# The 32-partition loads of v issued from ScalarE's queue

## The chip, the core and the metric

The kernel runs on one core of a Trainium2 chip. The core has a matrix engine (TensorE, PE in the rows; its weight loads are PEld), three engines for elementwise work (VectorE = DVE, ScalarE = ACT, GpSimd = POOL) and SyncE (SP), which here does nothing but issue transfers. Each engine takes its own instructions strictly in order and waits on semaphores for the others. Transfers between DRAM and the on-chip memory run on 16 DMA engines; an engine that issues a transfer only starts it. The metric is the device time of one execution, in microseconds.

## The reference, cut to what matters

```python
def _attn_ref(q, k, v):                 # 4 batches, 8 heads, 768 positions, 64 per head
    k_sum = k.reshape(B, H, nb, block, D).max(axis=3)      # 24 blocks of 32 positions
    v_sum = v.reshape(B, H, nb, block, D).mean(axis=3)
    scores_l = scale * np.matmul(q, k.transpose(0, 1, 3, 2))
    mask_l = np.abs(pos[:, None] - pos[None, :]) < 16
    scores_s = scale * np.einsum('bhsd,bhnd->bhsn', q, k_sum) + np.log(block)
    scores_all = np.concatenate([np.where(mask_l, scores_l, -1e9), scores_s], axis=-1)
    a = softmax(scores_all)
    return np.matmul(a, np.concatenate([v, v_sum], axis=2))

def _moe_ref(x, w_in, w_spatial, b_spatial, w_out):        # x: 4 x 768 x 512
    h = np.maximum(x @ w_in, 0.0)
    u, v = h[..., :512], h[..., 512:]
    v_n = (v - mean(v)) / np.sqrt(var(v) + 1e-06)
    v_s = np.einsum('ts,bsd->btd', w_spatial, v_n) + b_spatial[None, :, None]
    return (u * v_s) @ w_out
```

Each query sees the 15 positions on either side of it and all 24 block summaries; the result goes through a gated layer that also mixes positions.

## The kernel before

The attention is cut into 24 groups: 4 batches, 3 chunks of 256 query positions, 2 groups of four heads. A chunk is four blocks of 64 queries. For such a block the keys and values stand as 120 rows: 64 positions, 24 block summaries, and 32 further positions (the window reaches 16 past the block on either side). The value tile `ve` of a group therefore has 120 partitions: 0 to 63 are loaded from DRAM (256 KB), 64 to 87 hold the block means, which ACT writes, and 88 to 119 are loaded from DRAM (128 KB). Two such tiles, `ve0` and `ve1`, are used in turn, one for each group of heads, so a load into one has to wait until the product that reads it (the matmuls at L501, tile `x`) is done for the group before.

For each group PE makes the scores (`s`, L441), DVE and ACT the softmax (`p`: DVE L457, ACT's exponentials L461, DVE or POOL the division L471), PE transposes (`t`, L482), ACT or DVE copies (`pt`), and PE forms `x` from `pt` and `ve`. The dense work stands between: `pv` and `pu` are the two halves of the first layer, `sp` and `q` the mixing of positions, `po` the last layer; all are L543 in the rows. `arena` holds the mixing weights, which in the later batches come back from a DRAM scratch (`scr`) piece by piece; `vt` is v transposed, from which DVE forms block sums (`vs_in`, L407) that PE transposes (`vmp`, L411).

All instructions are collected with a cost and a priority in a `Plan`, whose `order()` lays them out on the engines by the costs; they are then issued in the order of the planned starts, and each engine keeps that order. A transfer is entered by `dma(...)`, booked on SP. Its semaphore is one of eight lanes (DMAHW0 to DMAHW7 in the order's rows), handed out in turn; a transfer also waits until the transfer that had its lane before has landed. In the rows of the order, `[waits ...]` names the semaphores that an instruction waits for, without their values. Where a transfer waits for a lane on which the transfer eight places earlier ran, that lane is the one it takes over.

Of the kernel before, what the change touches and what calls it, by code (L numbers as in the profile page):

```python
# [25 lines left out]
QB = 64  # L26
BPU = 4
CH = QB * BPU
NCH = S // CH
WIN = 16  # L30
# [41 lines left out]
class Plan:  # L72
# [11 lines left out]
    def add(self, engs, fn, pri, w=(), r=(), port=False, xfer=0):  # L84


        op = Op()
        op.engs = engs if isinstance(engs, dict) else dict([engs])
        op.fn, op.pri, op.users, op.n = fn, pri + SHIFT.get(self.label, 0), [], len(self.ops)
        op.label = self.label  # L90
        op.port, op.xfer = port, xfer
        op.ready = op.start = op.end = 0
        after = set()
        for x in r:
            after.update(self.wrote.get(x, ()))
        for x in w:
            after.update(self.wrote.get(x, ()))
            after.update(self.read.get(x, ()))
        for x in w:
            self.wrote[x], self.read[x] = [op], []  # L100
        for x in r:
            self.read.setdefault(x, []).append(op)
        op.after = after
        op.bufs = list(dict.fromkeys(x for x in (*w, *r) if isinstance(x, Buf)))
        for x in (*w, *r):
            if isinstance(x, Buf) and not x.ops and x.tag in self.TURNS and x.args[4][:2] not in self.OUT_OF_TURN :
                self.turn.setdefault(x.tag, []).append(x)
                self.late.add(x)
            if isinstance(x, Buf) and op not in x.ops[-1:]:
                x.ops.append(op)  # L110
        self.ops.append(op)
        return op
# [77 lines left out]
def tile_local_summary_attention_gmlp(ctx: ExitStack, tc: tile.TileContext, qT, kext, vpad, vnat, vT, w_in, w_sp, b_rep, w_out, out):  # L190
    nc = tc.nc
    plan = Plan()
    add = plan.add
# [57 lines left out]
    qd = [const.tile([P, 2, BPU, QB], F32, name=f"qd{i}") for i in range(2)]  # L251
    ve = [const.tile([KW, BPU, 2 * P], F32, name=f"ve{g}") for g in range(2)]

    def dma(out_, in_, kb, pri, w=(), r=(), issue=420, rate=RATE):
        add(("SP", issue), lambda e: nc.sync.dma_start(out=out_() if callable(out_) else out_, in_=in_() if callable(in_) else in_), pri, w, r, xfer=kb * 1024 / rate)  # L255

    def eng(e):
        return dict(DVE=nc.vector, POOL=nc.gpsimd)[e]
# [9 lines left out]
    def split32(src, hi, lo, name, pri, key):  # L268

        n = src.shape[-1]  # L270
        st = Buf(moe, [P, GW], F32, "g", name)
        dma(lambda: st.t[:, :n], src, n * 0.5, pri, w=[st])
        add(("ACT", act_ns(n)), lambda e: nc.scalar.copy(out=hi, in_=st.t[:, :n]), pri, w=[key + "h"], r=[st])
        add(two_ns(n), lambda e: eng(e).tensor_sub(out=lo, in0=st.t[:, :n], in1=hi), pri, w=[key + "l"], r=[st, key + "h"], port=True)

    def split64(st, so, f, fo, src, hi, lo, pri, key, on_pe=False, at=0):

        if src.dtype != I64:
            n = src.shape[-1]
            dma(lambda: st.t[:, so:so + n], src, n * 0.5, pri, w=[(st, so), st])  # L280
            add(("ACT", act_ns(n)), lambda e: nc.scalar.copy(out=hi, in_=st.t[:, so:so + n]), pri, w=[key + "h"], r=[(st, so), st])
            add(two_ns(n), lambda e: eng(e).tensor_sub(out=lo, in0=st.t[:, so:so + n], in1=hi), pri, w=[key + "l"], r=[(st, so), st, key + "h"], port=True)
            return
# [6 lines left out]
        here = plan.label  # L290
        mark("l", key)
        dma(raw, src.bitcast(I32), n, pri + at, w=[kr], r=[st])
        plan.label = here

# [125 lines left out]
    def v_load(b, c, g, buf, pri):  # L420
        s0 = c * CH
        fs = slice(2 * g * P, 2 * (g + 1) * P)
        dma(ve[buf][:QB], vpad[b, s0:s0 + CH, fs].rearrange("(i p) f -> p i f", p=QB), 256, pri, w=[f"vea{buf}"], issue=620, rate=RATE_64)
        dma(ve[buf][SEG:],
            vpad[b, s0 + QB:s0 + QB + CH, fs].rearrange("(i p) f -> p i f", p=QB)[:2 * WIN], 128, pri, w=[f"veb{buf}"], issue=620, rate=RATE_32)

    p_sb, pt_sb = {}, {}

# [444 lines left out]
    def attention(*pair):  # L873
# [4 lines left out]
        def values(i, pri):  # L878
            mark("v", i)
            v_load(*group(i), pri - 4 + off("v", i))  # L880
# [120 lines left out]
WIRE, RATE, RATE_64, RATE_32 = 1900, 355.0, 215.0, 195.0  # L1001
# [58 lines left out]
```

## Time and profile before

| | us |
|---|---|
| median of 3 runs (398.48 to 401.46) | 398.81 |
| the profiled execution | 398.37 |
| span of its instructions | 396.6 |
| PE busy | 385.3 (97%) |
| DVE busy | 277.7 (70%) |
| ACT busy | 227.8 (57%) |
| POOL busy | 76.2 (19%) |
| all transfers, 90 MB on one data queue | 68.5% of 16 engines |

The profiled execution is 1.8 us longer than its span and 0.44 us below the median. The span begins with the first instruction; times of the rows are counted from there. PE begins with the scores of the first groups while the weights are still arriving, works in pieces until about 64 us, and from then on hardly pauses. Busy shares of PE include matmuls that keep its clock up (`warm`, up to 30 us).

### The profile page before, as it was taken

What the parts mean: (1) busy time and instruction counts of PE and PEld (TensorE: products, weight loads), DVE (VectorE), ACT (ScalarE), POOL (GpSimd) and SP (SyncE); (2) the same over time, 40 slices, a digit from 0 to 9 for tenths busy, and PEclk for the clock granted to TensorE, in tenths of its full rate; (3) what the DMA queues carried; (4) which work ended last, traced back from release to release, by engine and by line L of the source; (5) the groups of instructions that cost most, each with busy time, mean ns of one, the idle gap of its engine ahead of it and who ended that gap; (6) DMA issues with size and microseconds to landing.
All of it is one profiled execution on the core that took longest, in us unless ns stands there. A gap on an engine that the chain in (4) does not pass through costs nothing.

```text
span 396.6 us, 9130 instructions
## 1 busy us (share of the span) xinstructions
PE 385.3 (97%) x3372; PEld 335.6 (85%) x3372; DVE 277.7 (70%) x871; ACT 227.8 (57%) x672; POOL 76.2 (19%) x115
## 2 busy tenths in 40 slices
PE   8889998999999999999999999999999999999996
PEld 8657776888899888888998888889998888889985
DVE  3878998989899517999989553577797710687720
ACT  2789998679475625777473743543564821452221
POOL 4244686310001004334012000031000000510000
PEclk9989999999999999999999999999999999999999
DMA  8999999957596846699999910318897110089712
GB/s 284 296 400 335 327 249 266 362 190 206 182 354 237 224 161 232 204 298 328 339 328 361 260 43 0 135 62 323 301 355 245 56 57 0 28 305 364 284 62 99
DMA packets 34284, 90.64 MB, mean 229 GB/s; under 512 B 3264, under 2 KB 15040, under 8 KB 30912
## 3 DMA queue, kind: packets, MB, share of 16 engines
q1 hardware_dynamic: 34240, 90.06, 68.5%
q8 instruction: 27, 0.44, 0.5%
q14 instruction: 17, 0.14, 0.1%
HBM read 73.40 MB, written 16.65 MB: 227 GB/s over the span
## 4 chain that ended last, share of the span: by engine, by line
PE 74%; DMA 13%; DVE 7%; ACT 2%; SPq 1%; issue 1%; POOL 0%; DVEq 0%; ACTq 0%
PE po L543 17%; PE q L543 13%; PE pu L543 13%; PE pv L543 12%; PE sp L543 6%; DMA arena<-scr 4%; PE x L501 4%; PE t L482 4%; PE s L441 4%; DMA vt<-in_vT_dram 3%; DMA qd<-in_qT_dram 2%; DMA k<-in_kext_dram 2%; SPq L255 1%; DMA scr<-ct 1%; ACT p L461 1%
## 5 line engine op out<-in xcount | busy, mean ns | idle before, releaser
L461 ACT ACTIVATE p<-p,sums 128x120 f32<-128x120 f32 x192 | 73.5, 386 | 11.0 <-DVE sums L457 10.9
L457 DVE CUSTOM_DVE_ANT_0 p<-s,mask 128x120 f32<-128x120 f32 x192 | 41.9, 276 | 9.5 <-PE s L441 9.4
L543 PE MATMUL pu<-xh,win_h 128*128 128x256 f32 (+1 forms) x128 | 44.0, 344 | 0.0
L543 PE MATMUL pu<-xh,win_l 128*128 128x256 f32 (+1 forms) x128 | 43.1, 337 | 0.0
L543 PE MATMUL pu<-xl,win_h 128*128 128x256 f32 (+1 forms) x128 | 43.0, 336 | 0.0
L543 PE MATMUL po<-arena,gt 128*128 128x512 f32 (+1 forms) x168 | 40.6, 385 | 0.0
L543 PE MATMUL pv<-win_h,xh 128*128 128x512 f32 x96 | 39.2, 408 | 0.0
L543 PE MATMUL pv<-win_h,xl 128*128 128x512 f32 x96 | 37.6, 391 | 0.0
L543 PE MATMUL pv<-win_l,xh 128*128 128x512 f32 x96 | 37.5, 391 | 0.0
L543 PE MATMUL q<-arena,vnh 128*128 128x384 f32 x144 | 37.4, 340 | 0.1
L461 ACT ACTIVATION_READ_ACCUMULATOR p<-p,sums 128x1 f32 x192 | 36.3, 189 | 0.0
L543 PEld LDWEIGHTS po<-arena,gt 128*128 128x128 f32 x168 | 30.4, 188 | 6.0 <-issue 0.2
L582 POOL TENSOR_SCALAR mv<-mv 128x1 f32<-128x1 f32 x24 | 9.3, 386 | 135.2 <-DVE mv L578 134.5
L577 DVE BATCH_NORM_STATS2 mv<-vf 128x6 f32<-128x512 f32 x24 | 16.4, 683 | 23.1 <-ACT vf L574 23.0
L638 ACT ACTIVATE u<-pu 128x512 f32<-128x512 f32 (+1 forms) x32 | 15.6, 491 | 28.3 <-PE pu L543 28.2
L543 PE MATMUL q<-arena,wo_hl 128*128 128x384 f32 x144 | 29.2, 336 | 0.4 <-DMA arena<-scr 0.4
L261 ACT COPY pt<-t 120x512 f32<-120x512 f32 x38 | 21.8, 584 | 13.0 <-PE t L482 12.8
L482 PE MATMUL t<-ident,p 128*120 128x128 f32 x192 | 28.1, 278 | 1.1 <-POOL p L471 0.9
L482 PEld LDWEIGHTS t<-ident,p 128*120 128x120 f32 x192 | 22.5, 138 | 6.8 <-POOL p L471 2.2
L501 PEld LDWEIGHTS x<-pt,ve 120*64 120x64 f32 x768 | 23.6, 138 | 4.6 <-issue 3.1
L543 PEld LDWEIGHTS pu<-xh,win_h 128*128 128x128 f32 x128 | 24.3, 189 | 3.0 <-issue 0.2
L441 PE MATMUL s<-k,qd 64*64 64x120 f32 x768 | 23.9, 267 | 2.7 <-DMA qd<-in_qT_dram 2.0
(152 smaller groups left out, 872.2 us busy)
## 6 DMA issues: line engine op xcount, KB each, us to landing
arena<-scr SPq DMA_DIRECT2D x21, 1152.0 KB, 6.3
k<-in_kext_dram SPq DMA_DIRECT2D x16, 544.0 KB, 7.8
qd<-in_qT_dram SPq DMA_DIRECT2D x24, 256.0 KB, 7.9
ve<-in_vpad_dram SPq DMA_DIRECT2D x24, 256.0 KB, 8.2
out_dram<-ob SPq DMA_DIRECT2D x23, 256.0 KB, 2.0
arena<-scr SPq DMA_DIRECT2D x5, 1024.0 KB, 7.7
vt<-in_vT_dram SPq DMA_DIRECT2D x12, 384.0 KB, 4.1
scr<-ct SPq DMA_DIRECT2D x12, 384.0 KB, 4.3
```

The lines of the kernel that those rows point to most:

```text
L255: add(("SP", issue), lambda e: nc.sync.dma_start(out=out_() if callable(out_) else out_, in_=in_() if callable(in_) else in_), pri, w, r, ...
L261: (nc.scalar.copy if e == "ACT" else nc.vector.tensor_copy)(out=out_, in_=in_)
L441: nc.tensor.matmul(out=ps[a].t[r * QB:(r + 1) * QB, i * KW:(i + 1) * KW], lhsT=qt[hs, r, i], rhs=kts[r].t[hs, g * SEG:g * SEG + KW], start ...
L457: add(("DVE", 205), lambda e, i=i, mi=mi, a=a, pt=pt, k=k: nc.vector.tensor_tensor_reduce(out=at(pt, i), in0=ps[a].t[:, i * KW:(i + 1) * K ...
L461: add(("ACT", 380), lambda e, i=i, pt=pt, k=k: nc.scalar.activation(out=at(pt, i), in_=at(pt, i), func=AF.Exp, scale=-1.0, bias=st.t[:, 0, ...
L482: nc.tensor.transpose(out=ps.t[:KW, i * P:(i + 1) * P], in_=pt.t[:, i * KW:(i + 1) * KW], identity=ident)
L501: nc.tensor.matmul(out=x.t[a * D:(a + 1) * D, r * CH + n * QB:r * CH + (n + 1) * QB], lhsT=ve[buf][:, n, o:o + D], rhs=tt[a].t[:KW, n * P ...
L543: nc.tensor.matmul(out=ps.t[:, :n], lhsT=x, rhs=y, start=(first and j == i == 0), stop=(j == last and i == 2), skip_group_check=skip)
L577: nc.vector.bn_stats(out=mv.t[:, 2:], in_=vf.t)
L582: nc.gpsimd.tensor_scalar_add(out=mv.t[:, 1:2], in0=mv.t[:, 1:2], scalar1=EPS_LN)
L638: add(("ACT", act_ns(n)), lambda e: nc.scalar.activation(out=u.t[:, f, ts], in_=ps.t[:, :n], func=AF.Relu), pri, w=[(u, f, c)], r=[ps, u])
```

## The change

The function `dma` gets a parameter `queue`, and the second of the two loads in `v_load`, the one of 32 partitions and 128 KB, is issued by ACT (`nc.scalar`) and no longer by SP. The plan still books it on SP with the same costs, so the planned starts are what they were, and the instruction is put into ACT's order at its planned start.

```diff
-    def dma(out_, in_, kb, pri, w=(), r=(), issue=420, rate=RATE):
-        add(("SP", issue), lambda e: nc.sync.dma_start(out=out_() if callable(out_) else out_, in_=in_() if callable(in_) else in_), pri, w, r, xfer=kb * 1024 / rate)
+    def dma(out_, in_, kb, pri, w=(), r=(), issue=420, rate=RATE, queue=nc.sync):
+        add(("SP", issue), lambda e: queue.dma_start(out=out_() if callable(out_) else out_, in_=in_() if callable(in_) else in_), pri, w, r, xfer=kb * 1024 / rate)
@@ v_load
         dma(ve[buf][SEG:],
-            vpad[b, s0 + QB:s0 + QB + CH, fs].rearrange("(i p) f -> p i f", p=QB)[:2 * WIN], 128, pri, w=[f"veb{buf}"], issue=620, rate=RATE_32)
+            vpad[b, s0 + QB:s0 + QB + CH, fs].rearrange("(i p) f -> p i f", p=QB)[:2 * WIN], 128, pri, w=[f"veb{buf}"], issue=620, rate=RATE_32, queue=nc.scalar)
```

24 transfers leave SP's order and stand in ACT's; on PE, DVE and POOL nothing moves. Since the lanes are handed out in the order of issue over both queues, which lane a transfer takes, and which earlier one it so waits for, changes for most transfers behind the first few.

The first place is ACT's order in batch 1, chunk 2, in the softmax of the second group of heads (`p1_2_1_0` and `p1_2_1_1` are its two score tiles, `xh1_01_1` takes the result of the chunk before; rows with + are of after, with - of before).

```order
 L461 ACTIVATE p1_2_1_0_1570,sums_115<-p1_2_1_0_1570,sums_115 128x120 [waits DVE_49,Activation_49]
+L255 DMA ve0_140<-in_vpad_dram 32x4x256 [waits DMAHW7_49,DMAHW5_49]
 L461 ACTIVATE p1_2_1_0_1570,sums_115<-p1_2_1_0_1570,sums_115 128x120 [waits DVE_49] x3
+L255 DMA ve1_141<-in_vpad_dram 32x4x256 [waits DMAHW7_49,DMAHW1_49,PE_49]
 L461 ACTIVATE p1_2_1_1_1583,sums_115<-p1_2_1_1_1583,sums_115 128x120 [waits DVE_49,Activation_49]
 L461 ACTIVATE p1_2_1_1_1583,sums_115<-p1_2_1_1_1583,sums_115 128x120 [waits DVE_49] x3
-L523 CAST xh1_01_1_1339<-x1_1_1_1502 128x2x256 [waits PE_49]
+L523 CAST xh1_01_1_1339<-x1_1_1_1502 128x2x256
```

Two loads now stand among the exponentials. The load of `ve1` takes over lane 7, for which it has to wait.

The second place is SP's order at the same time; `scr8` is a store of weights to the scratch, `qd0` a load of queries, `k2_0` and `k2_1` keys of the next batch.

```order
 L255 DMA scr8_137<-wo_hl_128 128x2x512 [waits DMAHW6_49,DVE_49]
 L255 DMA ve0_140<-in_vpad_dram 64x4x256 [waits DMAHW7_49,PE_49]
-L255 DMA ve0_140<-in_vpad_dram 32x4x256 [waits DMAHW0_49]
-L255 DMA ve1_141<-in_vpad_dram 64x4x256 [waits DMAHW1_49,PE_49]
-L255 DMA ve1_141<-in_vpad_dram 32x4x256 [waits DMAHW2_49]
-L255 DMA qd0_138<-in_qT_dram 128x512 [waits DMAHW3_49,PE_49]
-L255 DMA k2_0_1622<-in_kext_dram 128x1088 [waits DMAHW4_49]
-L255 DMA k2_1_1631<-in_kext_dram 128x1088 [waits DMAHW5_49]
-L255 DMA k2_2_1639<-in_kext_dram 128x1088 [waits DMAHW6_49,PE_49]
-L255 DMA k2_3_1651<-in_kext_dram 128x1088 [waits DMAHW7_49]
+L255 DMA ve1_141<-in_vpad_dram 64x4x256 [waits DMAHW0_49,PE_49]
+L255 DMA qd0_138<-in_qT_dram 128x512 [waits DMAHW2_49,DMAHW1_49,PE_49]
```

The two small loads are gone from SP's order. The transfer that holds lane 7 until it has landed is SP's load of `ve0` with 64 partitions, in the second row, in both kernels; before, `k2_3` took the lane over from it, eight transfers later.

The third place is ACT's order in batch 1, chunk 0, near the end of the stage in which the weights arrive (`xh0_2_0` takes the last result of batch 0, `vmp1_0` block means of batch 1).

```order
 L574 ACTIVATE vf0_2_911<-pv0_2_768 128x512
 L273 CAST arena_125<-ws3_700 128x768 [waits DMAHW0_49]
-L523 CAST xh0_2_0_943<-x0_2_0_886 128x512 [waits PE_49]
+L255 DMA ve0_140<-in_vpad_dram 32x4x256 [waits DMAHW3_49,DMAHW1_49,PE_49]
+L523 CAST xh0_2_0_943<-x0_2_0_886 128x512
 L413 ACTIVATE ve0_140<-vmp1_0_913 24x4x128 [waits PE_49]
 L461 ACTIVATE p1_0_1_0_966,sums_115<-p1_0_1_0_966,sums_115 128x120 [waits DVE_49] x3
+L255 DMA ve1_141<-in_vpad_dram 32x4x256 [waits DMAHW5_49,PE_49]
 L261 COPY pt1_0_0_0_992<-t1_0_0_0_976 120x512 [waits PE_49,Activation_49]
```

On SP the load of `ve0` with 32 partitions stood four transfers behind that of `vt1_2`; now it is on the other queue.

## Rows read from the trace of the kernel before

**Rows 1.** The page: engines with busy time, share of the span and instructions; then the DMA queues with packets, MB and the time of their packets as a share of 16 engines.

```profile
PE 385.3 (97%) x3372; PEld 335.6 (85%) x3372; DVE 277.7 (70%) x871; ACT 227.8 (57%) x672; POOL 76.2 (19%) x115
...
q1 hardware_dynamic: 34240, 90.06, 68.5%
```

**Rows 2.** Who waited for whom, PE alone: total us, times, longest.

```profile
PE s L441 <- DMA qd<-in_qT_dram: 2.0, 1, 2.0
...
PE vmp L411 <- DVE vs_in L407: 1.4, 1, 1.4
...
PE x L501 <- DMA ve<-in_vpad_dram: 0.5, 1, 0.5
...
PE q L543 <- DMA arena<-scr: 0.4, 1, 0.4
PE t L482 <- DVE p L471: 0.2, 1, 0.2
```

**Rows 3.** Stretches: from and to, length, busy time and instructions of PE, PEld, DVE, ACT, POOL, then the granted clock, the share of the DMA engines and GB/s.

```profile
30.00:40.00 10.00, 9.12 (x154) 7.24 (x147) 8.55 (x43) 9.95 (x36) 4.32 (x5) 1.00 1.07 330
40.00:50.00 10.00, 9.89 (x128) 7.54 (x127) 9.49 (x33) 9.92 (x35) 6.15 (x5) 1.00 1.03 333
50.00:60.00 10.00, 9.49 (x130) 7.38 (x131) 9.83 (x34) 9.31 (x29) 8.71 (x7) 1.00 1.07 245
60.00:70.00 10.00, 8.56 (x67) 6.92 (x66) 8.78 (x30) 8.89 (x28) 5.92 (x7) 1.00 1.04 271
...
167.00:175.00 8.00, 8.00 (x141) 7.44 (x138) 7.16 (x29) 4.64 (x17) 1.51 (x3) 1.00 0.96 309
202.00:213.00 11.00, 10.57 (x65) 9.72 (x64) 10.10 (x39) 7.34 (x27) 3.03 (x3) 1.00 1.02 357
278.00:288.00 10.00, 10.00 (x165) 9.51 (x164) 7.27 (x38) 5.62 (x23) 0.00 (x0) 1.00 0.93 308
```

**Rows 4.** The chain that ended last, in order of time, at the end of the stage in which the weights arrive: start, length, what.

```profile
51.80 11.51 DMA vt<-in_vT_dram
...
63.33 0.96 DVE vs_in L407
...
64.43 0.28 PE vmp L411
```

**Rows 5.** DMA issues of the stretch 58.5 to 60: line, size, median us from issue to landing; and SP's timeline there (start, length, what).

```profile
ve<-in_vpad_dram SPq DMA_DIRECT2D x1, 256.0 KB, 8.1
ve<-in_vpad_dram SPq DMA_DIRECT2D x1, 128.0 KB, 8.2
...
58.60 1.25 SPq L255 DMA_DIRECT2D ve<-in_vpad_dram  x2
```

**Rows 6.** All instructions on the tile `ve`: the issues on SP, with ns of one, shortest, median and longest; and SP's timeline at one issue of 128 KB that had waited for its lane.

```profile
L255 SPq DMA_DIRECT2D ve<-in_vpad_dram x48: 327/601/1927, 4.5 to 304.2; - x48
...
46.95 0.33 SPq L255 DMA_DIRECT2D ve<-in_vpad_dram  x1
```

**Rows 7.** SP's timeline around 104, and the issue of the first of these four loads with its time to landing.

```profile
104.40 3.40 SPq L255 DMA_DIRECT2D ve<-in_vpad_dram  x4
...
ve<-in_vpad_dram SPq DMA_DIRECT2D x1, 256.0 KB, 6.7
```

**Rows 8.** ACT's timeline at the place of the first piece of order: the first exponential of `p1_2_1_1`, the end of the fourth, and the cast behind it.

```profile
108.99 0.38 ACT L461 ACTIVATE p<-p,sums 128x120 f32<-128x120 f32 x1
...
110.41 0.19 ACT L461 ACTIVATION_READ_ACCUMULATOR p<-p,sums 128x1 f32 x1
110.51 0.57 ACT L523 CAST xh<-x 128x512 fp32r<-128x512 f32 x1
```

**Rows 9.** DVE's timeline right behind, and PE's transposes of the same tiles.

```profile
110.92 0.17 DVE L466 TENSOR_SCALAR sums<-sums 128x9 f32<-128x9 f32 x1
111.12 0.20 DVE L467 RECIPROCAL sums<-sums 128x8 f32<-128x8 f32 x1
111.25 0.64 DVE L524 TENSOR_TENSOR xl<-x,xh 128x512 fp32r<-128x512 f32 x1
111.80 1.22 DVE L471 TENSOR_TENSOR p<-p,sums 128x480 f32<-128x480 f32 x2
...
113.41 1.04 PE L482 MATMUL t<-ident,p 128*120 128x128 f32 x8
```

**Rows 10.** The stretch from 167: ACT's timeline at the place of a small load, the chain that ended last, and DVE's timeline with its idle time in brackets.

```profile
167.09 0.51 ACT L703 CAST ct<-ct 128x384 fp32r<-128x384 f32 x1
...
167.67 5.87 DMA scr<-ct
...
173.66 0.56 DVE L700 TENSOR_TENSOR ct<-w,w 128x384 f32<-128x384 f32 x1 [0.77 <-DMA scr<-ct]
...
180.89 1.19 PE t L482 x8
```

**Rows 11.** The chain that ended last around 202 to 213.

```profile
199.12 0.60 SPq L255
...
202.01 10.77 DMA arena<-scr
...
212.92 1.11 PE q L543 x5
```

**Rows 12.** The issue of a piece of `arena` at 278.28 with its time to landing, and PE's first matmul that reads it.

```profile
arena<-scr SPq DMA_DIRECT2D x1, 1152.0 KB, 9.1
...
287.69 0.51 PE L543 MATMUL q<-arena,vnh 128*128 128x384 f32 x2
```

## The prediction

> **What bounds the kernel now.** I read the page's engine lines first, then PE's own waits, then the stretches, then the chain that ended last wherever PE had waited. PE is busy for 385.3 of 396.6 us [rows 1], and the list of its waits is short: the waits on transfers and on DVE that it names add to about 4.5 us in the whole execution [rows 2]. From about 64 us on PE runs without a pause in almost every stretch. The time is therefore PE's work plus the pauses put into it: whatever delays PE by a microsecond after 64 us is paid in full, and a faster queue can win back only pauses that exist. Up to 70 us the second limit is the transfers: the DMA engines are at a share of 1.03 to 1.07 for 40 us, while ACT is at 9.95 and 9.92 of 10 between 30 and 50 [rows 3]. That stage ends on a transfer: `vt` is issued at 51.80, lands 11.51 later, DVE reduces it in 0.96, and PE, which had paused 1.4 for it, goes on at 64.43 [rows 2, 4].
>
> **What the change removes.** SP loses 24 issues. At the median of 601 ns that is 14.4 us of SP's time [rows 6], but SP is not what lasts: its transfers wait for lanes, for buffers that PE still reads, or for the backlog. At 51.80 the backlog is 11.5 us [rows 4]; a transfer that is issued half a microsecond earlier lands where the bytes ahead of it let it land. One wait of PE is on `ve` itself, 0.5 us in the first stage [rows 2]; the small load may now land earlier there, but PE then only waits longer for `vt` at 64.43. Removed: 0 us, and with the issue that stands on the chain at 199.12 (0.60) up to 0.35 at one place, counted below.
>
> **What it adds to ACT: the issue.** No row shows an issue on ACT. The nearest are the same loads on SP: 0.33 us where SP had just waited and nothing stood before it, 0.60 as the median, 1.93 at worst [rows 6]. Below nothing is excluded, since ACT's sequencer has one more thing to do. I take 0.33, because on ACT the loads stand alone between computations. In the first stage four of them fall where ACT is full, two near 34 to 37 us and two near 48 to 50: 4 x 0.33 = 1.3 us later. The cover is PE's pause of 1.4 before 64.43 [rows 2]: the delayed work of ACT, DVE and PE has to be done before `vt` lands, and just fits. So 0 at 0.33; above 0.36 each further 0.1 costs 0.4. Elsewhere ACT has 43% idle time, and an issue costs nothing unless the exponentials behind it are awaited.
>
> **What it adds to ACT: the waits.** Each load waits on ACT for its buffer, for its lane's last transfer, and for the earlier load of the same tile; everything behind it on ACT waits too. I went through the 24 places and compared, in the trace, when ACT reaches the place with when the awaited things had come. At 23 of them they had come, or come within some 0.7 us where nobody waits for ACT. The other is the first piece of order, among the exponentials of batch 1, chunk 2. The load of `ve1` takes over lane 7 from SP's 64-partition load of `ve0`. That was issued at 104.40 and took 6.7 us, so it landed at 111.1 [rows 7]. ACT reaches the place at 108.99 [rows 8]. With the issue of 0.33 behind it ACT goes on at 111.4: 2.4 us late. Behind it are four exponentials, whose sums are ready at 110.6 now and 113.0 then. DVE's L466 began at 110.92 [rows 8, 9], so 0.3 is free there, and 2.1 remains; but DVE's `xl` at 111.25 needs ACT's cast at 110.51, which will end at about 113.5, so L471 begins near 114.1 instead of 111.80 and its two halves end near 114.7 and 115.3. PE begins the transposes at 113.41, 1.04 us for the eight, four for each half [rows 9]: it will begin at 114.8 and reach the second four at 115.4 instead of 113.9. That is 1.5 to 1.6 us of pause, and 0.1 more at the next pair of tiles, whose exponentials are late by the same amount: **1.7**. Bounds: 1.0 if the landing comes 0.6 earlier, 2.6 if it comes later because the other queue now takes a share, and the issue costs 0.60.
>
> **What it adds to the transfers.** In the rows all data stand on one queue, q1 [rows 1], and they land in order of issue. A second queue lets the small load run beside what is waiting on the first, so 128 KB are moved ahead of a backlog that they used to close. The small load itself is then early, which nobody needs; what was ahead of it is late. The price is 128 KB at the rate of the stretch, or the distance between two landings. At 58.60 the pair landed at 58.60 + 8.1 and 59.25 + 8.2, 0.7 apart (59.25 is the second issue of the two in 1.25 us) [rows 5]; 128 KB at 271 GB/s are 0.48 [rows 3].
> - At 64.43: the load that is issued at 59.25 now will be issued by ACT near 60, while `vt` is still under way until 63.3. **0.6** (0 to 0.7).
> - At 173.5: DVE waits 0.77 for a landing, issued at 167.67 [rows 10]. ACT is free from 167.6 to 170.4 and will issue its load of `ve0` there, ahead of it. 128 KB at 309 GB/s are 0.42 [rows 3]. The chain runs from that landing over DVE to PE's transposes at 180.89, for which PE waited 0.2 already [rows 2, 10]. **0.5** (0 to 0.8).
> - At 212.9: the piece of `arena` issued at 202.01 lands 10.77 later and PE waited 0.4 for it [rows 2, 11]. The load of `ve0` used to stand behind it and will be issued by ACT near 203.8: 128 KB at 357 GB/s are 0.37 [rows 3]. The issue taken from SP at 199.12 can give 0.35 back. **0.3** (-0.35 to 0.65).
> - At 287.7: the piece issued at 278.28 lands at 287.4 and is read at 287.69 [rows 12], 0.3 to spare; the small load comes near 284.3 and needs 0.43 at 308 GB/s [rows 3]. **0.2** (0 to 0.5).
>
> What a page says of this: the Trainium skill, "DMA: Bandwidth & Descriptors", section "Queues, rings and completion order", has each DMA engine take turns between the queues that have work, a packet at a time. With one data queue before, no row shows it. By that rule the four terms hold at their full price; if the engines served the queues strictly by time of issue, all four would be 0.
>
> **The sum.** 0.6 + 1.7 + 0.5 + 0.3 + 0.2 = 3.3 us of new pauses on PE, 0 for the issues. From the profiled execution of 398.37 that gives 401.7. Against the median of 398.81, which is 0.44 above that execution, it is 0.7% more. Less than 1%, about 4 us, is hardly told from no change by runs of this kernel, whose three runs lie between 398.48 and 401.46.
>
> **The rivals.**
> - *The second queue carries its loads for nothing.* The share of the DMA engines is 1.07 both at 330 and at 245 GB/s [rows 3], so a full share is not a full rate, and two queues could overlap better. Then the two small loads near 47 to 49 no longer stand ahead of `vt`, which could land up to 1.4 earlier (2 x 0.7), as much as PE's pause there; the four terms are 0, and the wait of ACT keeps its 1.7: 398.4 - 1.4 + 1.7 = **398.7**. Without the wait of ACT it is 397.0. A gain of over 1% would need more than 3.6 us, nearly all of PE's waits in rows 2, in one go. For it: the uneven rates. Against it: the uneven rates also follow the kinds of transfers. The same page of the Trainium skill, section "Issuing engines are not separate DMA queues", says that transfers of all issuing engines run on the same 16 DMA engines and interleave, so that spreading saves only issue time. By that rule this rival falls; no run so far shows it.
> - *The issue is dear on ACT.* This one ends on the slower side. Its place is ACT between 34 and 50 us, its price four issues, and it decides from 0.36 us for one. At 0.8, between SP's median and its worst [rows 6], ACT is 3.2 late, PE's pause covers 1.4, and 1.8 remains in place of the 0.6; the wait at 109 grows by 0.5 to 2.2; the others stay: 1.8 + 2.2 + 1.0 = 5.0, **403.4**. At 1.0 it is 2.6 + 2.4 + 1.0 = 6.0, 404.4, and exponentials that are awaited at other steps would add some tenths each. For it: SP needs 0.60 wherever issues follow each other, and SP still issues its 64-partition loads at these times. Against it: the single issue of 0.33.
> - *The lane at 109 is free in time.* If `ve0` lands before ACT comes, 1.7 falls away: 400.0. It would have to land 2 us earlier, with the same issue at 104.40; little speaks for it.
>
> That the change does not do what it says can be left out: the 24 loads do stand in ACT's order.
>
> **How the numbers follow.** Forecast, 400.2 to 403.2: 0.45. Loads for nothing, 397 to 399.9: 0.25, of it 0.04 for a gain of over 1%. Issue dear, 402.8 to 407: 0.25. Lane free, about 400: 0.05. Slower by over 1% (above 402.8) is the dear issue and some 0.13 of the forecast's upper part: 0.38. Faster by over 1% (below 394.8): 0.04. Within 1%: 0.58. The range from 398.0 to 405.5 leaves out about half of the loads for nothing and the top of the dear issue, 2 in 10.
>
> **What would show it.** In the profile of the changed kernel: on ACT a pause of about 2 us among the exponentials near 110, ended by the landing of `ve`, and a new wait of PE's `t` of 1.5 us or more near 114; `vt` landing 0.5 or so later before PE's `vmp`; PE's wait for `arena` near 213 at 0.7 or so. A second data queue must appear with 24 x 128 KB = 3.1 MB. ACT's issues should last 0.33; if they last 0.6 and more, the dear issue decides, and PE's pause before `vmp` shows it with ACT late. I am wrong if `vt` lands earlier than now, or if PE does not pause near 114.

## The result, and the profile after

The changed kernel takes 401.90 us, the median of 19 runs (398.42 to 407.30); the kernel before takes 398.26 in 19 runs beside it (394.69 to 401.46). The ratio is 1.0102, with a 95% interval from 1.0077 to 1.0126: 4.1 us slower, between 3.1 and 5.0. Forecast were 401.7 and 3.3 us. Ratios here compare the undisturbed runs of two kernels and medians are over all runs, so the two can differ by some tenths of a per cent. The profiled execution of after took 401.07 with a span of 399.3, 2.7 more than before's in both.

The page of after: PE and ACT, and the data queues (packets, MB, share of 16 engines).

```profile
PE 385.3 (96%) x3372; PEld 334.9 (84%) x3372; DVE 279.2 (70%) x871; ACT 228.3 (57%) x672; POOL 76.8 (19%) x115
...
q1 hardware_dynamic: 30784, 86.91, 65.6%
q10 hardware_dynamic: 3456, 3.15, 3.5%
```

PE's busy time is that of before to the tenth [rows 1]; all that was added is idle time of PE. The second data queue, q10, carries the 3.1 MB that were forecast.

All instructions on `ve`: the issues, with ns of one (shortest, median, longest).

```profile
L255 ACTq DMA_DIRECT2D ve<-in_vpad_dram x24: 317/318/555, 1.6 to 308.2; - x24
L255 SPq DMA_DIRECT2D ve<-in_vpad_dram x24: 595/607/1206, 4.3 to 305.7; - x24
```

An issue on ACT takes 0.32, SP's short value [rows 6] and not its median. The rival of the dear issue falls.

Whom PE waited for in after (total, times, longest).

```profile
PE t L482 <- DVE p L471: 2.8, 2, 1.5
PE s L441 <- DMA qd<-in_qT_dram: 1.8, 2, 1.3
...
PE pu L543 <- DVE sums L457: 0.9, 1, 0.9
...
PE vmp L411 <- DVE vs_in L407: 0.5, 1, 0.5
```

Against [rows 2]: the wait of `t` for DVE's `p` has grown from 0.2 to 2.8, in two places, one of them the 1.5 us near 114 that was forecast; the wait of `vmp` has fallen from 1.4 to 0.5, which was not. The wait for `arena` near 213, forecast to grow from 0.4 to 0.7, is not in the list any more.

Near 109, ACT's timeline, then DVE's and PE's behind it (idle time before, in brackets).

```profile
107.52 0.19 ACT L461 ACTIVATION_READ_ACCUMULATOR p<-p,sums 128x1 f32 x1
109.68 0.32 ACTq L255 DMA_DIRECT2D ve<-in_vpad_dram  x1
110.10 0.40 ACT L461 ACTIVATE p<-p,sums 128x120 f32<-128x120 f32 x1 [2.39 <-DMA qd<-in_qT_dram]
...
111.63 0.56 ACT L523 CAST xh<-x 128x512 fp32r<-128x512 f32 x1
```

```profile
111.75 0.17 DVE L466 TENSOR_SCALAR sums<-sums 128x9 f32<-128x9 f32 x1 [2.21 <-ACT p L461]
...
112.83 1.22 DVE L471 TENSOR_TENSOR p<-p,sums 128x480 f32<-128x480 f32 x2
```

```profile
113.62 1.20 PE L482 MATMUL t<-ident,p 128*120 128x128 f32 x8 [1.52 <-DVE p L471]
```

The chain of the forecast stands there link by link: ACT is done at 107.71, stands until its load goes out at 109.68 and begins the next exponential 2.39 after the last; DVE's L466 waits 2.21 for it; PE pauses 1.52. The profile puts ACT's wait down to `qd`. The transfer that holds lane 7 fits better: SP issued its 64-partition load of `ve0` at 102.94, and it landed 6.6 later, at 109.5. In all four traces that have this load among the exponentials (here, and three of the kernels below) ACT issued it 0.1 us behind that landing, whether the landing took 5.3, 6.5, 6.6 or 6.9.

```profile
ve<-in_vpad_dram SPq DMA_DIRECT2D x1, 256.0 KB, 6.6
```

The chain that ended last, at the end of the first stage and near 168.

```profile
61.97 0.88 DVE vs_in L407
62.98 0.28 PE vmp L411
...
168.49 7.69 DMA scr<-ct
176.30 0.56 DVE ct L700
...
183.54 1.19 PE t L482 x8
```

PE's `vmp` began 1.45 earlier than in before, and the store at 168.49 landed 1.82 later after its issue than in [rows 10]. In this one execution the change seems to win 1.5 in the first stage and to lose 2.5 between 117 and 190. Both readings had to be tested.

### The profile page after: what moved, and what is told of

Its sections match the earlier page's. It is cut to its first block, busy times and chain, and to the rows that moved or that the text cites. A ratio compares the mean times of both kernels' runs of the same rounds, so it can differ in the third digit from the quotient of the medians.

```text
span 399.3 us, 9138 instructions
## 1 busy us (share of the span) xinstructions
PE 385.3 (96%) x3372; PEld 334.9 (84%) x3372; DVE 279.2 (70%) x871; ACT 228.3 (57%) x672; POOL 76.8 (19%) x115
## 4 chain that ended last, share of the span: by engine, by line
PE 73%; DMA 16%; DVE 6%; ACT 3%; issue 1%; POOL 0%; SPq 0%; ACTq 0%; DVEq 0%
PE po L543 17%; PE q L543 15%; PE pu L543 13%; PE pv L543 12%; DMA wi<-in_w_in_dram 8%; PE sp L543 5%; PE x L501 4%; PE t L482 4%; DMA qd<-in_qT_dram 3%; PE s L441 3%; DMA scr<-ct 2%; DMA k<-in_kext_dram 2%; DMA arena<-scr 2%; ACT p L461 1%; DVE mv L577 1%
## 5 line engine op out<-in xcount | busy, mean ns | idle before, releaser
L461 ACT ACTIVATE p<-p,sums 128x120 f32<-128x120 f32 x192 | 73.6, 387 | 16.5 <-DVE sums L457 11.5
```

Of the source, the lines that this page charges most:

```text
L461: add(("ACT", 380), lambda e, i=i, pt=pt, k=k: nc.scalar.activation(out=at(pt, i), in_=at(pt, i), func=AF.Exp, scale=-1.0, bias=st.t[:, 0, ...
```

## The experiments

Four hypotheses were to be told apart: the loss is ACT's wait for lane 7 (the forecast's largest term); it is what the second queue makes late; it is spread over all places; and the first stage gains. Most kernels change the one condition at the end of this line (shown from its middle on); its number counts the 24 loads by their groups, 0 to 7 in the first stage, 10 and 11 near 109, 14 and 15 near 168 to 174, 16 and 17 near 201 to 206. Loads that the condition leaves out are issued by SP as before. A ratio is the time divided by that of before in runs beside it, with its 95% interval in brackets.

```diff
-            ... issue=620, rate=RATE_32, queue=nc.scalar)
+            ... issue=620, rate=RATE_32, queue=nc.scalar if 6 * b + 2 * c + g in (10, 11) else nc.sync)
```

### The place at 109

Only the two loads of this place on ACT (the condition is `in (10, 11)`):

> Only the two small loads of batch 1, chunk 2 (issued near 106 and 110) come from ACT's queue. Theory: this place alone carries the wait of ACT, PE pauses 0.6 to 3 at 113 to 117 and the ratio is 1.003 to 1.006. Rival (the wait needs the other loads on ACT, or PE's pause is made up later): 0.999 to 1.002.

Measured was a ratio of 1.0049 (1.0015 to 1.0083), 1.9 us. ACT stands as in after, and PE behind it:

```profile
109.62 0.32 ACTq L255 DMA_DIRECT2D ve<-in_vpad_dram  x1
110.04 0.40 ACT L461 ACTIVATE p<-p,sums 128x120 f32<-128x120 f32 x1 [2.10 <-DVE sums L457]
```

```profile
113.57 1.19 PE L482 MATMUL t<-ident,p 128*120 128x128 f32 x8 [1.36 <-DVE p L471]
```

The place costs what was forecast, with the other 22 loads on SP.

All loads on ACT, the one that waited moved behind 14 ACT instructions (`LATER` is 13; the loop then runs over `ops`):

```diff
+    ops = plan.order()
+    late = [o for o in ops if str(o.label) == "v_11"][1]
+    at = ops.index(late)
+    behind = [n for n, o in enumerate(ops) if n > at and o.eng == "ACT"][LATER]
+    ops.insert(behind, ops.pop(at))
```

> All 24 small loads come from ACT's queue as in after, but the one that waited for lane 7 near 109 (ve1 of batch 1, chunk 2) stands fourteen ACT instructions later in the order, behind the exponentials and a copy, where it is issued near 115 and nobody waits for ACT. Theory (ACT's wait for the lane is the largest part of the loss): PE has no pause at 113 to 117 against before (it had 1.9 in after, 3.7 and 0.6 in the two others with this load among the exponentials), and the time is 1.3 to 2.1 us below after's, a ratio to before of 1.004 to 1.007. Rival (the pause goes elsewhere, or the loss lies in the transfers): PE pauses at 113 to 125 all the same, or the ratio stays at 1.009 to 1.012.

The load goes out behind a copy, and PE's `t` follows without an idle time:

```profile
113.36 0.59 ACT L261 COPY pt<-t 120x512 f32<-120x512 f32 x1 [0.23 <-PE t L482]
113.43 0.32 ACTq L255 DMA_DIRECT2D ve<-in_vpad_dram  x1
```

```profile
112.29 1.03 PE L482 MATMUL t<-ident,p 128*120 128x128 f32 x8
```

The pause is gone, and none comes up to 117. The ratio is 1.0079 (1.0039 to 1.0118), some 0.9 us below after, less than the 1.3 to 2.1 expected; the intervals allow either, and no gain too.

All loads on ACT but these two (`not in (10, 11)`):

> All small loads come from ACT's queue but the two of batch 1, chunk 2 (issued near 106 and 110 in after), which stay on SP's. Theory: ACT no longer stands behind lane 7 at 109, PE has no new pause of 1.7 at 113, and the span is 1.9 shorter than after's 399.3: 397.4, a ratio to before of 1.002, to after 0.995. Rival: DVE or PE are late at 113 for another reason (the second queue makes queries and keys late there), and PE pauses at 113 to 117 by 1 us or more all the same; the span stays at 398.5 or above.

No pause at 113 here either, but the ratio is 1.0118 (1.0044 to 1.0193, four runs) and not 1.002. So the place at 109 is a cost of its own and not the whole, and the time of these few runs does not show what its removal gives back.

### The other places

The loads of the first stage alone (`< 8`):

> Only the eight small loads of the first stage (issued up to 62 us) come from ACT's queue; the other sixteen stay on SP's. Theory, from the trace of after: the first stage gains, since vt lands earlier and PE's vmp begins 1.45 us earlier, and nothing is lost behind it. The span is then 1.2 to 1.7 us shorter than before's 396.6, and the ratio to before is 0.996. Rival, the prediction's own term for this stage: the early vt of after is the scatter of one execution, PE's vmp begins at 64.4 or later (65.0 by the prediction), and the ratio is 1.000 to 1.002.

The ratio is 1.0025 (0.9985 to 1.0065): neither gain nor loss can be seen. `vmp` did begin at 62.40, as the theory had it, and the time did not follow.

The sixteen others (`>= 8`):

> Only the sixteen small loads behind the first stage come from ACT's queue. Theory, from the trace of after: what costs time lies here, 1.9 us of PE's pauses near 113 to 117 (ACT waits for its lane) and 2.4 near 175 to 190; PE's vmp begins at 64.4 as before; the span is 400.5 to 401 and the ratio to before 1.010 to 1.011. If the pauses near 175 come from ACT's longer code (the fetch of 8 KB at 169.09 in after), the eight loads that ACT lacks in front of it move this fetch to some 172 us, and the pauses there may change by a microsecond either way; if they come from the small load that overtakes, they are 2.4 again. Rival, the prediction's sum: no gain to lose in the first stage, 1.7 near 113 and 0.5 near 181: the span is 399.6 and the ratio 1.007.

The ratio is 1.0113 (1.0041 to 1.0186, four runs). By this the loss lies in these sixteen, though its size is open: the median of the four is 0.6% above that of before. And `vmp` began at 63.30 with the first stage as in before, so its early start is no work of the second queue.

Six loads, the pair near 109 among them (`8 <= ... < 14`):

> Six of the small loads come from ACT's queue, those issued between 87 and 128 us in after (batch 1, chunks 1 and 2, and batch 2, chunk 0), among them the one at 109.7 for which ACT waits for lane 7. The others stay on SP's queue. Theory: ACT's wait costs PE 0.6 to 1.9 us at 113 to 117 (it did so in the two profiles that had this load on ACT, after and the later sixteen, and in none of the four others), and no transfer on which PE waits stands near; the ratio to before is 1.003 to 1.005. Rival: the wait is not what costs the time (the kernel with these two loads back on SP was timed at 1.012 with an interval from 1.004), and the ratio is 1.000 within 0.002.

The ratio is 1.0034 (1.0003 to 1.0065); the pair near 109 alone had 1.0049. Its profiled execution took 404.04, the longest of its 12 runs, and is left out of the table below; it shows a price of the pause that the forecast lacked (last section).

The last ten (`>= 14`):

> The last ten small loads come from ACT's queue, those issued behind 167 us; the others stay on SP's. Theory (the second queue puts 128 KB ahead of stores and reads of the scratch on which DVE and PE wait): PE's pauses at 175 to 190, 213 and 366 to 372 grow by some 0.7 each on average, and the ratio is 1.005 to 1.007. Rival: what the traces show there is scatter from one execution to the next (PE's delay between 175 and 190 was 2.5, 0.9 and -0.3 with these loads on ACT, and 1.0, 0.0 and -0.6 with them on SP), and the ratio is 1.000 to 1.002.

The ratio is 1.0035 (0.999 to 1.0081); the median of its 12 runs, 401.32, lies 0.9% above that of before. The time does not decide. Its trace shows a second place where ACT stands for a transfer:

```profile
201.66 0.32 ACTq L255 DMA_DIRECT2D ve<-in_vpad_dram  x1
202.03 0.40 ACT L461 ACTIVATE p<-p,sums 128x120 f32<-128x120 f32 x1 [1.45 <-DVE p L471]
```

The load waited for `qd`, issued at 195.59 and landed 6.05 later, at 201.64, before it went out at 201.66. PE paused 1.9 at `q` near 212.5, for DVE; that ACT's wait led to it is not shown.

Two loads (`in (14, 15)`):

> Only the two small loads issued near 168 and 174 in after (batch 2, chunk 1) come from ACT's queue, ahead of the store of scr2 and the reads behind it for which DVE waits at 173. Theory A (this place is what remains when the places at 109 and at 201 to 206 are undone, which left a ratio of 1.007): DVE's wait for the store grows, PE loses 1 or more between 153 and 182 against 0.6 on average in the kernels with these loads on SP, and the ratio is 1.003 to 1.006. Theory B (one overtaken transfer of 128 KB, the prediction's 0.5): PE loses 0.5 to 1.2 there in one execution, which is within the scatter, and the ratio is 1.000 to 1.002.

The ratio is 1.0016 (0.9983 to 1.0049): theory B, or nothing. The 2.5 us that after's trace lost here are not what the change does here as a rule.

All but the two places where ACT stands (`not in (10, 11, 16, 17)`):

> All small loads come from ACT's queue but four: those of batch 1, chunk 2 (ACT's wait for lane 7 near 109) and those issued near 201 and 206 in after, for which ACT waited 1.45 in one profile and behind which the reads of keys and of arena land later. Theory (these two places are the whole loss, 2 and 1 us): the ratio is 0.999 to 1.003. Rival (every place on the second queue costs a little, by transfers made late for DVE and PE): the ratio is 1.005 or more, and PE's waits for arena and for DVE between 175 and 215 stay above those of before.

The ratio is 1.0071 (1.003 to 1.0112): the theory falls. The two places are not the whole loss; 1.2 to 4.5 us lie in loads of which no group tested alone shows them clearly.

The kernel before, with its code on ACT made longer (six copies at each of four places; only the lines that add them are shown):

> The kernel before, all loads on SP's queue, with 24 small ACT instructions (128x1 copies into a tile that nobody reads, at 138 to 146 us in ACT's idle time) put into ACT's code ahead of the stretch at 168 to 182 us. It asks for the cause of the loss there without moving any load. Theory (code loading): ACT's next 8 KB of code, fetched at 177 us in before and at 169.09 in after, are fetched near 168 to 170 here too, on a DMA engine that still has the store of scr2 to do; that store lands 1 us or more later than its 5.87 after issue, DVE's wait for it at 173.7 grows from 0.77 to 1.5 to 2.7, and PE loses 0.7 to 2 us between 175 and 182: the span is 397.3 to 398.6. Rival (the small load overtakes): as no load is moved, the store lands as before, DVE waits 0.8 and the span stays 396.6 within 0.3.

```diff
+        if op.eng == "ACT" and str(op.label) in PAD_AT:
+            for _ in range(6):
+                nc.scalar.copy(out=pad, in_=mhalf)
```

The labels are those of the first four outputs. The ratio is 0.9991 (0.9942 to 1.004). This is inconclusive: the padding moved the fetch too far, to 174 us instead of 168 to 170, so the question was not put. That code is fetched in this stretch can be read in the queues between 168 and 170 (before first, then after):

```profile
q8 instruction: 1, 0.02, 5.9%
```

```profile
q8 instruction: 1, 0.02, 7.9%
q14 instruction: 1, 0.01, 7.1%
```

7.9% and 7.1% of 16 engines over 2 us are 2.5 and 2.3 us on one engine. Whether this made after's store late was not settled; before has the first of the two fetches as well.

### Twice the bytes, and another engine

The larger load of each pair on ACT, the smaller one on SP:

> The other load of each pair, 256 KB in 64 partitions, comes from ACT's queue and the one of 128 KB stays on SP's: the same number of issues on ACT, twice the bytes on the second queue. Theory (overtaking costs by bytes): what the second queue costs behind 170 us doubles from some 2 to 4, the wait of ACT near 109 stays, and the ratio is 1.014 to 1.018. Rival (the cost lies in ACT's waits and issues, whatever the bytes): 1.008 to 1.012.

```diff
-        ... issue=620, rate=RATE_64)
+        ... issue=620, rate=RATE_64, queue=nc.scalar)
...
-            ... issue=620, rate=RATE_32, queue=nc.scalar)
+            ... issue=620, rate=RATE_32)
```

The ratio is 1.009 (1.0052 to 1.0128): as after, at twice the bytes. A cost by bytes on the second queue is not borne out.

All small loads on GpSimd (`queue=nc.gpsimd`):

> All 24 small loads come from GpSimd's queue; ACT issues nothing, and these loads take no lane from the others. Theory (ACT's waits and the second queue each cost something): the pause at 113 is gone, what the second queue costs later stays, and the ratio is 1.004 to 1.008, if GpSimd's own waits cost nothing. Rival 1 (only waits and lanes cost, the second queue nothing): 0.997 to 1.001. Rival 2: GpSimd stands before these loads until PE has read the tile, with divisions behind it for which PE's transposes wait in the first stage; then PE's vmp begins at 66 or later and the ratio is 1.005 to 1.015 from there.

The ratio is 1.0108 (1.0061 to 1.0154). There is no pause at 113, and `vmp` begins at 64.11, so neither ACT's wait nor rival 2 made this; rival 1 falls by the time. Of PE's waits those for `arena` have grown, from 0.4 to 4.7:

```profile
PE q L543 <- DMA arena<-scr: 2.7, 2, 1.8
...
PE po L543 <- DMA arena<-scr: 2.0, 1, 2.0
```

Taking the waits from ACT does not save the change: with the same loads on GpSimd's queue the reads of `arena` come late; the one read near 213 landed 12.9 after its issue. How much of this is usual stays open: the profiled execution, 405.61, is the longest of its six, and by the columns of the table below it loses 1.0 up to 117, 1.8 from there to 213 and 4.6 behind it.

### One table over the traces

Each trace is one execution, so a stretch is read over all of them. The times are those between the starts of the same matmuls in PE's timeline: `vmp` (64.43 in before), `t` (116.90, inside the group that begins at 116.36), `q` (189.62), `q` (212.92) and the last. A star marks a stretch whose loads are on ACT: the first eight, the one that waited near 109 (among the exponentials), those near 168 and 174, near 201 and 206, and the six behind.

```
loads on ACT         vmp at   to 117   to 190   to 213   to the end
none (before)        64.43    52.47    72.72    23.30    180.04
none, padded         61.79    52.47    72.15    22.61    181.37
first eight          62.40*   52.51    73.74    23.83    180.61
109 alone            63.09    54.22*   73.37    22.61    179.94
168, 174 alone       65.67    52.52    73.50*   23.50    179.86
later sixteen        63.30    53.08*   72.38*   23.35*   179.81*
last ten             62.00    52.43    72.71*   25.33*   179.88*
all but 109          64.59*   52.43    73.61*   24.21*   180.89*
all but 109, 201-206 64.36*   52.45    73.84*   23.62    179.64*
all, 109 moved       63.33*   52.45    75.06*   24.62*   180.31*
all (after)          62.98*   54.38*   75.18*   22.96*   180.16*
mean with a star     63.53    53.89    73.75    24.09    180.12
mean without         63.38    52.47    73.00    23.24    180.36
difference            0.15     1.42     0.75     0.85    -0.24
```

The second column is the clear one: eight traces without the load among the exponentials lie between 52.43 and 52.52, three with it between 53.08 and 54.38. In the others the scatter is as large as the difference: `vmp` begins anywhere from 61.79 to 65.67, whichever queue the first loads are on.

## Why the prediction was right, and where its steps were not

- **The sum.** 3.3 us were forecast and 4.1 (3.1 to 5.0) measured; the table's differences add to 2.9. Its largest term is shown; that the number fits as well owes something to luck, for of the other terms some were too large and one too small, and 1.1 of the measured 4.1 stands in no column.
- **ACT's wait for lane 7, 1.7.** Right in place, mechanism and size: 1.9 in after's trace, 1.4 on average over the table, 1.9 in time with this pair alone, and no pause when the load is moved. (The forecast's own times, 114.8 for 113.41 and 115.4 for 113.9, give 1.4 to 1.5 and with the next tiles 1.6.) Each link had its row beforehand: the lane in the order, the landing and ACT's arrival in [rows 7, 8], DVE and PE behind in [rows 9]. That it is the only place where ACT stands was wrong: at the load near 201 to 206 that waited for `qd`, ACT stood 1.45, 1.64 and 1.87 before its next exponential in three traces, 0.65 in after and not at all in the fifth. Whether PE lost by that is not shown.
- **The issue, 0.33.** Right: 0.32.
- **64.43, 0.6.** Wrong, near 0. The step that failed was to take PE's pause of 1.4 before `vmp` [rows 2] as something that the kernel has. Of the ten other traces in the table each shows 0.5 there, with the first loads on either queue. In after `vt` was issued at 50.73 and landed 9.3 later, at 60.0, and DVE took it up at 61.97 only:

```profile
vt<-in_vT_dram SPq DMA_DIRECT2D x1, 384.0 KB, 9.3
```

  In the nine others too `vt` had landed 0.3 to 3.1 before DVE came. So what bounds that place is DVE's queue of work, and before's profiled execution was one in which `vt` came late. Nor did the loads on ACT delay `vt`: it landed 7.5 to 9.4 after its issue in the five traces with the first eight on ACT, and 7.9 to 11.5 in the six with them on SP. The forecast had named an earlier `vt` as a sign of being wrong, and after's trace has it; of this term it was one. The rival of the loads for nothing would have read that trace as its own success; the same early `vmp` with the first loads on SP (61.79 to 63.30 in four traces) refutes it.
- **173.5, 0.5.** The table has 0.8, with a scatter of 1: not told apart from the forecast. The store landed 4.8, 5.87, 6.12 and 6.87 after its issue in the four traces with the loads of this place on SP, and 5.4, 5.81, 6.32, 6.39, 6.56, 7.69 and 7.83 in the seven with them on ACT: 0.7 later on average, and the two sets overlap.
- **212.9, 0.3.** Too small. The piece of `arena` landed 9.5, 9.8, 10.41, 10.43, 10.77 and 11.04 after its issue in the six traces with the loads of 201 to 206 on SP, and 11.0, 11.49, 11.72, 12.34 and 13.1 in the five with them on ACT. That is 1.6 more on average. The piece was also issued 0.6 earlier (counted from the `q` at which the third column ends), so 1.0 is left as a later arrival, where 128 KB at the rate of the stretch were 0.37. The direction was right, and the price by bytes was not; why it is nearly three times that was not found. What PE paid there is 0.85 by the table, with a scatter as large; in after itself PE did not wait. A gain from the issue taken from SP did not show in PE's time.
- **287.7, 0.2.** Nothing is seen. In after ACT issued its load 5.6 behind the piece of `arena` (286.45 against 280.86), about as forecast (6.0), and the piece landed 7.9 after its issue, not later than the 9.1 of [rows 12]. Over the table it is 7.7 to 9.3 with these loads on ACT and 7.9 to 9.4 on SP. Why a small load delays a large one near 213 and not here stays open.
- **The two places near 110 and 201 as a full account.** My later theory, not the forecast's; the kernel with all but these four stayed at 1.007. What makes up the rest stays open.

Of the two sections of the Trainium skill, "DMA: Bandwidth & Descriptors", the one on issuing engines agrees with the runs: the first eight loads on a second queue show no gain (1.0025, with 0.9985 as its lower end), nor did GpSimd's queue. The turns between queues, of "Queues, rings and completion order", agree in sign with the later landing of `arena` near 213, but `vt` and the piece near 288 did not land later; the runs do not show the turns themselves.

No kernel of this study beats the one before by more than its interval.

## What to carry to other kernels

An issue moved to a computing engine brings its waits along, the lane's among them; the 0.3 us of the instruction did not matter, a transfer still under way did. Look for the place where that engine arrives before the transfer it must wait for, and whether what stands behind is awaited; placing the issue behind that work removed the pause here, though what it gained in time was within the noise. Before a pause in one profiled execution is used as cover or as prize, look whether it is there in a second. And compare a transfer's arrival with the work that needs it, not its time from issue alone: of the 1.6 us at `arena`, 0.6 came from an earlier issue.

## What the runs showed of the hardware

A pause can cost twice. In the kernel with loads 8 to 13 on ACT, PE paused 1.79 before `t` at 115.91. PE's windows there: 105 to 113, 113 to 116, 116 to 121, 121 to 130 (the granted clock is the third figure from the end).

```profile
105.00:113.00 8.00, 8.00 (x133) 7.58 (x128) 4.83 (x35) 3.44 (x13) 0.00 (x0) 1.00 1.06 290
113.00:116.00 3.00, 1.21 (x6) 0.69 (x5) 1.87 (x5) 3.00 (x16) 0.00 (x0) 1.00 1.03 363
116.00:121.00 5.00, 5.00 (x21) 3.90 (x22) 4.64 (x11) 1.97 (x9) 0.00 (x0) 0.66 0.92 321
121.00:130.00 9.00, 9.00 (x146) 8.80 (x148) 7.87 (x20) 4.37 (x11) 2.03 (x2) 1.00 0.32 109
```

Right behind the pause the granted clock is 0.66 of full speed over five microseconds, part of them at 1.2 GHz instead of 2.4. From this `t` to the next PE takes 4.67 (115.91 to 120.58), where before takes 2.95 (113.41 to 116.36): a further 1.7. The kernel on GpSimd shows it a second time, behind the pause at 382, and not behind the one at 215:

```profile
215.48 0.76 PE L543 MATMUL q<-arena,wo_hl 128*128 128x384 f32 x3 [1.82 <-DMA arena<-scr]
382.06 2.60 PE L543 MATMUL po<-arena,gt 128*128 128x512 f32 x6 [2.01 <-DMA arena<-scr]
```

```profile
382.00:387.00 5.00, 4.95 (x15) 3.95 (x16) 0.56 (x1) 0.70 (x2) 0.00 (x0) 0.66 0.00 0
215.40:220.40 5.00, 4.92 (x32) 4.42 (x34) 3.68 (x9) 0.88 (x3) 1.38 (x1) 1.00 1.03 366
```

After the pause of 1.52 in after and that of 1.90 in the last ten on ACT the clock stayed at 1.00 as well. So the length of a pause alone does not tell whether it is paid twice; what does was not tested here.
